# Pooled keys written once, as a ring of nine heads, and transposed by two DMAs from its first and second slot on

## Chip, cores, metric

One core of one Trainium2 chip. The metric is the device time of one execution in microseconds, lower is better. Before the change it was 290.78 us (median of three runs, 290.66 to 291.47). In what follows TensorE is PE in the profile (PEld are its weight loads), VectorE is DVE, ScalarE is ACT, GpSimd is POOL, and SyncE, which only issues DMAs here, is SP. Matmul results lie in PSUM, the rest of this kernel's tiles in SBUF; both are memories on the chip. All runs compared are in the fast state.

## The reference

```python
# q, k, v: 8 batches x 8 heads x 576 rows x 64;  w_in: 512 x 2048;  w_out: 2048 x 512
k_p = k.reshape(B, H, Sp, 8, D).mean(axis=3)          # 576 rows -> 72 pooled rows
v_p = v.reshape(B, H, Sp, 8, D).mean(axis=3)
attn = softmax(q @ k_p^T / sqrt(D));  x = attn @ v_p   # x as 4608 tokens x 512
h = x @ w_in
out = (h * cos(h)) @ w_out
```

## The kernel before

The 4608 tokens go through the two large products in nine tiles of 512, t = 0 to 8. During tile t the attention of batch b = t + 1 is done, and GpSimd pools the keys and values of the batch after. Five pieces matter here.

GpSimd pools by three rounds of pairwise adds. The last round of the keys is done twice, so that each head stands twice, side by side, before the transpose:

```python
def pool_rest(b, which):
    s, add = half_sums, nc.gpsimd.tensor_tensor
    for h in range(0, H, 4):
        add(out=s[:, h:h + 4, 0:2, :], in0=s[:, h:h + 4, 0:2, :], in1=s[:, h:h + 4, 2:4, :], op=ADD)   # L155
    if which == "k":
        for slot in range(2):
            add(out=kp2[b % 2][:Sp, :, slot, :], in0=s[:, :, 0, :], in1=s[:, :, 1, :], op=ADD)          # L158
    else:
        s = s.rearrange("p (j a) t d -> p j a t d", a=2)
        add(out=v_part(b), in0=s[..., 0, :], in1=s[..., 1, :], op=ADD)                           # L161
```

SyncE transposes the doubled keys in one DMA, so that every head's keys lie on both halves of the partitions (a score matmul takes the half on which its queries happen to lie):

```python
def k_transpose(b):
    nc.sync.dma_start_transpose(out=kk[b % 2], in_=kp2[b % 2].rearrange("p h s d -> p (h s d)"))
```

VectorE forms h * cos(h) from PSUM (L358), and sums and differences of the parts of g for a product scheme with seven instead of eight block products. These sums (L388) have **both inputs in SBUF**:

```python
nc.vector.tensor_mul(out=o, in0=ps, in1=c)                                  # L358: ps in PSUM
nc.vector.tensor_tensor(out=out[:, f0:f1], in0=x, in1=y, op=op)             # L388: x, y in SBUF
```

In each tile the sums begin after the fourth of eight chunks, while GpSimd, which works ahead through its queue, finishes the values and loads what comes next:

```python
for n, fp in enumerate(up_order(t)):
    up_mm(t, fp, ...); up_g(t, fp, between)                                  # L344; L354, L358
    if 0 < t and 3 <= n < 6:
        put_gs(*[(k, 0) for k in (((3,), (1,), ()) if t == 1 else ((1, 2), (3,), (4,)))[n - 3]])
    if 0 < t and b < B:
        if n == 0:
            q_transpose(b); k_transpose(b)
        elif n == 2:
            pool_rest(b, "v")
            if b + 1 < B:
                nc.gpsimd.tensor_copy(out=gate, in_=kk[b % 2][0:1, 0, 0:1])  # L580
                load_q(b + 1); load_kv(b + 1, "v", v)
# ... seven block products (L422), attention of batch b between them; then, after tile 0 (conditions cut) ...
nc.gpsimd.tensor_copy(out=gate, in_=g4[0:1, HF - 1, 0:1])                    # L703
pool_first(b + 1, "k")                                                       # L149
load_kv(b + 2, "k", k)
pool_rest(b + 1, "k")
pool_first(b + 1, "v")
```

The 1x1 gate copies hold GpSimd's queue, and the loads in it, until something else is done.

The softmax here doesn't subtract the row's maximum and nothing guards it: scores larger than these inputs give would overflow.

Of the kernel before, what the change touches and what calls it, by code (L numbers as in the profile page):

```python
# [10 lines left out]
BF16 = mybir.dt.bfloat16  # L11
ACTF = mybir.ActivationFunctionType
ADD = mybir.AluOpType.add
# [7 lines left out]
def kernel(  # L21
# [9 lines left out]
    nc = tc.nc  # L31
    B, H, S, D = q.shape
    Sp = S // POOL
# [22 lines left out]
    wpool = ctx.enter_context(tc.tile_pool(name="wpool", bufs=1))  # L56
# [17 lines left out]

    SpA = -(-Sp // 16) * 16
    kk = [wpool.tile([128, H, SpA], BF16, name=f"kk{i}") for i in range(2)]
    kp2 = [wpool.tile([SpA, H, 2, D], BF16, name=f"kp2{i}") for i in range(2)]

    vz = [wpool.tile([Sp, KCH, 4, D], BF16, name=f"vz{i}") for i in range(2)]

# [30 lines left out]
    def load_kv(b, which, src):  # L111

        st = kv_tile()[:Sp, 0:H * POOL * D].rearrange("p (h t d) -> p h t d", h=H, t=POOL)
        nc.gpsimd.dma_start(out=st.rearrange("p h t d -> p h (t d)"),
                            in_=src[b].rearrange("h (p t) d -> p h (t d)", t=POOL))
        staged[which, b] = st

    def load_q(b):
        q_tile(b)
        load_even(staged["q", b], b, q)  # L120
# [13 lines left out]
    half = (slice(0, 64), slice(64, 128))  # L134

    def v_part(b):
        return vz[b % 2][:, :, 0:4:3, :]

    def put_kk(b, ps, pj0, pj1, copy):
        dst = kk[b % 2].rearrange("p (j a) n -> p j a n", a=2)  # L140
        for a in range(2):
            for r in range(2):
                copy(out=dst[half[r], pj0:pj1, a, 0:Sp], in_=ps[half[a]])

    def pool_first(b, which):

# [4 lines left out]
    def pool_rest(b, which):  # L151

        s, add = half_sums, nc.gpsimd.tensor_tensor
        for h in range(0, H, 4):
            add(out=s[:, h:h + 4, 0:2, :], in0=s[:, h:h + 4, 0:2, :], in1=s[:, h:h + 4, 2:4, :], op=ADD)  # L155
        if which == "k":
            for slot in range(2):
                add(out=kp2[b % 2][:Sp, :, slot, :], in0=s[:, :, 0, :], in1=s[:, :, 1, :], op=ADD)  # L158
        else:
            s = s.rearrange("p (j a) t d -> p j a t d", a=2)  # L160
            add(out=v_part(b), in0=s[..., 0, :], in1=s[..., 1, :], op=ADD)  # L161

    def pool_k_mm(b, bank, pj0, pj1):

        kb = staged["k", b]
        ps = bank[:, 0:(pj1 - pj0) * Sp].rearrange("p (j n) -> p j n", n=Sp)
        for pj in range(pj0, pj1):
            for t in range(ROW):
                for rows in half:
                    nc.tensor.matmul(ps[rows, pj - pj0, :], lhsT=kb[rows, pj, t, :], rhs=groups[rows, t, :],  # L170
                                     start=(t == 0), stop=(t == ROW - 1))
        return lambda copy: put_kk(b, ps, pj0, pj1, copy)
# [8 lines left out]
                              in_=pair[:Sp, :, 0:KCH * D].rearrange("p a (j d) -> p a j d", j=KCH))  # L181

    def k_transpose(b):
        nc.sync.dma_start_transpose(out=kk[b % 2], in_=kp2[b % 2].rearrange("p h s d -> p (h s d)"))


    QB = KCH * ROW // 2
# [7 lines left out]
    def q_transpose(b):  # L195
        qT_tile(b)
        nc.sync.dma_start_transpose(out=att["qT", b], in_=q_flat(b))

    def q_transpose_mm(b, bank, g0, g1):

        if ("qT", b) not in att:
            qT_tile(b)
        ps = bank.bitcast(BF16)[:, 0:(g1 - g0) * 128].rearrange("p (g n) -> p g n", n=128)
        for g in range(g0, g1):
            nc.tensor.matmul(ps[:, g - g0, :], q_flat(b)[:, g * 128:(g + 1) * 128], identity, is_transpose=True)
        return lambda copy: copy(out=att["qT", b][:, g0:g1, :], in_=ps)

    def ex_col(u, i):

        (c0, n), (h0, nh) = u  # L210
        return (i // 2 % 2 * (nh // 2) + i // 4 * 2 + i % 2) * n

    def scores(b, u, pair):
        scores_mm(b, u, pair)
        scores_exp(b, u, pair)

    def scores_mm(b, u, pair):
        (c0, n), (h0, nh) = u

        for i in [i + 2 * a for k in range(0, nh, 4) for i in (k, k + 1) for a in range(2)]:  # L220
            bank, c = divmod(ex_col(u, i), nh * n // 2)
            pj, hp = divmod(h0 + i, 2)
            g, r = divmod(ROW * pj + ORDER[c0 // 64], 2)
            nc.tensor.matmul(pair[:Sp, bank, c:c + n].rearrange("p (g n) -> p g n", n=64),  # L224
                             lhsT=kk[b % 2][half[r], h0 + i, 0:Sp],
                             rhs=att["qT", b][half[r], g:g + n // 64, hp * 64:hp * 64 + 64])

    def scores_exp(b, u, pair):
# [99 lines left out]
    def up_order(t):  # L328
        n = FFCH // 2
        return range(n) if t < FIRST else [i + a * n // 2 for i in range(n // 2) for a in range(2)]  # L330
# [7 lines left out]
    def up_mm(t, fp, k0=0, k1=KCH):  # L338

        h = up_bank(t, fp)  # L340
        for j in range(2):
            fc = 2 * fp + j
            for ki in range(k0, k1):
                nc.tensor.matmul(h[j] if h is obanks else h[:, j, :], lhsT=w_in_sb[fc // 4][:, ki, (fc % 4) * 128:(fc % 4 + 1) * 128],  # L344
                                 rhs=xT[:, ki, t * TILE:(t + 1) * TILE],
                                 start=(ki == 0), stop=(ki == KCH - 1))

    def up_g(t, fp, between=()):
        h = up_bank(t, fp)
        cos = msb.tile([128, 2, TILE], FP32, name="cos", tag="cos", bufs=2)  # L350
        g = g_sb[:, 2 * fp:2 * fp + 2, :]
        parts = [(h[j], cos[:, j], g[:, j]) for j in range(2)] if h is obanks else [(h, cos, g)]
        for ps, c, _ in parts:
            nc.scalar.activation(out=c, in_=ps, func=ACTF.Sin, bias=half_pi[:, :1])  # L354
        for put, copy in between:
            put(copy)
        for ps, c, o in parts:
            nc.vector.tensor_mul(out=o, in0=ps, in1=c)  # L358
# [31 lines left out]
    def put_gs(*kis):  # L390
        for k, i in kis:
            put_g(k, i)
# [79 lines left out]
    for rows in half:  # L472
# [12 lines left out]
                  for x in (g1, g2)]  # L485
    groups = g3.rearrange("p f n -> p (f n)")[:, 0:ROW * Sp].rearrange("p (t n) -> p t n", t=ROW)
    nc.vector.tensor_tensor(out=dist, in0=row_of.unsqueeze(2).to_broadcast([128, ROW, Sp]),
                            in1=first_of.unsqueeze(1).to_broadcast([128, ROW, Sp]), op=mybir.AluOpType.subtract)
# [6 lines left out]
    gate = consts.tile([1, 1], BF16, name="gate")  # L495
# [12 lines left out]
    load_even(staged["v", 1], 1, v)  # L508
    nc.gpsimd.memset(vz[1], float(POOL))
    for i in range(2):  # L510
        nc.gpsimd.memset(kp2[i], 0.0)
    for cg in (2, 1, 3):
        load_w_out(cg)

# [37 lines left out]
    for t in range(NT):  # L552
        b = t + 1
# [4 lines left out]
        for n, fp in enumerate(up_order(t)):  # L558
            up_mm(t, fp, 2 if n < 2 else 0)
            between = ()  # L560
            if t == 0:
                if fp == 4:
                    puts = pool_k_mm(1, obanks[0], 0, 2), pool_k_mm(1, obanks[1], 2, 4)
                elif fp in (5, 6):
                    g0 = 9 * (fp - 5)
                    puts = q_transpose_mm(1, obanks[0], g0, g0 + 5), q_transpose_mm(1, obanks[1], g0 + 5, g0 + 9)
                if fp in (4, 5, 6):
                    puts[0](vec)
                    between = ((puts[1], act),)
            up_g(t, fp, between)  # L570
# [4 lines that stand above are left out]
                    q_transpose(b)  # L575
                    k_transpose(b)
                elif n == 2:
                    pool_rest(b, "v")
                    if b + 1 < B:
                        nc.gpsimd.tensor_copy(out=gate, in_=kk[b % 2][0:1, 0, 0:1])  # L580
                        load_q(b + 1)
                        load_kv(b + 1, "v", v)
            if n == 2:
                while stores:
                    stores.pop(0)()
# [39 lines left out]
        else:  # L625
# [11 lines left out]
            def scores_of(*parts):  # L637
                for part in parts:
                    scores_mm(*part)
                for part in parts:  # L640
                    scores_exp(*part)
# [52 lines left out]
        if b + 1 < B:  # L694
            if t == 0:
                load_kv(b + 1, "k", k)
                load_q(b + 1)
                load_kv(b + 1, "v", v)
                put_weights(0, nc.gpsimd, (3, 2, 4))
                put_weights(1, nc.gpsimd, (1,))  # L700
# [4 lines that stand above are left out]
            if b + 2 < B:  # L705
# [3 lines that stand above are left out]
# [28 lines left out]
```

## Time and profile before

The lines are in the prediction below; here is what they come to.

| | before |
|---|---|
| time, median of 3 | 290.78 us |
| PE busy, share of the span | 276.1 us, 96% |
| GpSimd busy, idle at gate L703 | 151.3 us, 36.0 us |
| length of tiles 2, 3, 4, 5, 6 | 30.07, 29.63, 29.64, 29.62, 28.95 us |
| mean of the L388 call; free call | 804 ns; about 690 ns |

Tile lengths run from the first up-projection matmul of a tile to that of the next. Tiles 2 to 6 hold the same matmuls, so their lengths can be set against each other; that is the reading on which everything below rests.

### The profile page before, as it was taken

How to read it: one execution, taken by the hardware profiler on the slowest of the kernel's cores; microseconds unless marked ns; L12 is line 12 of the kernel's file. 1: busy time of each engine (PE TensorE's matmuls, PEld its weight loads, DVE VectorE, ACT ScalarE, POOL GpSimd, SP SyncE). 2: the span in 40 equal slices, each digit the busy share in tenths (PEclk: the TensorE clock that was granted, in tenths of full speed). 3: DMA queues.
4: the chain of work that ended last, by engine and by line, in shares of the span. 5: the costliest groups of instructions: out<-in, count | busy, mean ns of one | idle time of the engine just before them, and what ended most of it. 6: DMA issues, size and time to landing. Idle time of an engine off the chain costs nothing.

```text
span 288.7 us, 5827 instructions
## 1 busy us (share of the span) xinstructions
PE 276.1 (96%) x2338; PEld 175.9 (61%) x2360; DVE 218.5 (76%) x314; ACT 164.5 (57%) x193; POOL 151.3 (52%) x150
## 2 busy tenths in 40 slices
PE   7889999999999899999999999999999999999994
PEld 2545454447864597449744884488448844874683
DVE  6458747899949995799569956995699569756962
ACT  3886798378157635763566556565566556436600
POOL 8563079997799369934994399529920000000000
PEclk9999999999999999999999999999999999999999
DMA  7999999793999957996789668972660261015014
GB/s 158 197 206 206 207 205 212 121 189 40 155 122 177 181 93 118 165 170 110 116 160 175 112 104 154 184 125 55 125 145 3 55 137 29 2 23 122 2 36 109
DMA packets 57545, 36.12 MB, mean 125 GB/s; under 512 B 35248, under 2 KB 53168, under 8 KB 57520
## 3 DMA queue, kind: packets, MB, share of 16 engines
q0 software_dynamic: 19744, 18.07, 40.0%
q1 hardware_dynamic: 37136, 17.18, 30.4%
q10 hardware_dynamic: 640, 0.52, 0.8%
q8 instruction: 18, 0.29, 0.4%
q14 instruction: 7, 0.06, 0.1%
HBM read 36.70 MB, written 9.44 MB: 160 GB/s over the span
## 4 chain that ended last, share of the span: by engine, by line
PE 64%; DVE 17%; DMA 12%; ACT 3%; POOL 2%; issue 1%; DVEq 0%; POOLq 0%
PE obank L422 27%; PE bank L344 24%; DVE g_sb L358 9%; DVE g L388 7%; DMA w_out_sb<-in_moe_w_out_dram 7%; DMA w_in_sb<-in_moe_w_in_dram 5%; PE obank L361 4%; ACT cos L354 3%; PE bank L224 3%; PE obank L344 2%; PE bank L286 2%; PE bank L259 1%; PE bank L422 1%; DVE o_two L438 1%; POOL q_b L95 1%
## 5 line engine op out<-in xcount | busy, mean ns | idle before, releaser
L344 PE MATMUL bank<-xT,w_in_sb 128*128 128x512 bf16 x495 | 113.5, 379 | 2.1 <-DVE g_sb L358 1.2
L354 ACT ACTIVATE cos<-bank,half_pi 128x1024 f32<-128x1024 f32 x64 | 70.4, 1114 | 58.5 <-PE bank L344 51.8
L344 PEld LDWEIGHTS <-w_in_sb 128*128 128x128 bf16 x576 | 56.0, 98 | 67.9 <-issue 2.9
L358 DVE TENSOR_TENSOR g_sb<-bank,cos 128x1024 bf16<-128x1024 f32 x64 | 77.0, 1219 | 24.9 <-ACT cos L354 24.8
L149 POOL TENSOR_TENSOR half_sums<-kv_st 72x512 f32<-72x512 bf16 x48 | 54.8, 1168 | 0.8 <-issue 0.2
L231 ACT ACTIVATE ex<-bank 72x1024 bf16<-72x1024 f32 (+1 forms) x40 | 35.0, 929 | 35.2 <-PE bank L224 35.1
L422 PEld LDWEIGHTS <-g 128*128 128x128 bf16 x512 | 47.9, 98 | 7.0 <-issue 1.2
L422 PE MATMUL obank<-w,g 128*128 128x256 bf16 x368 | 42.8, 272 | 0.4 <-DVE p_sb L436 0.2
L422 PEld LDWEIGHTS <-g_sb 128*128 128x128 bf16 x384 | 36.6, 98 | 8.7 <-DVE g_sb L358 2.2
L155 POOL TENSOR_TENSOR half_sums<-half_sums 72x512 f32<-72x512 f32 x24 | 30.9, 1309 | 0.1
L422 PE MATMUL obank<-w_out_sb,g_sb 128*128 128x256 bf16 x240 | 29.4, 273 | 1.1 <-DVE g_sb L358 1.1
L388 DVE TENSOR_TENSOR g<-g_sb 128x1024 bf16<-128x1024 bf16 x32 | 25.7, 804 | 0.5
L703 POOL COPY gate<-g 1x1 bf16<-1x1 bf16 x5 | 0.9, 180 | 36.0 <-DVE g L388 36.0
L270 DVE TENSOR_TENSOR xT<-bank,inv 64x256 bf16<-64x256 f32 x14 | 5.9, 422 | 15.2 <-ACT inv L266 15.1
L291 DVE TENSOR_TENSOR x_rows<-bank,inv_rows 128x512 bf16<-128x512 f32 x24 | 16.6, 692 | 0.8
L158 POOL TENSOR_TENSOR kp<-half_sums 72x512 bf16<-72x512 f32 x12 | 15.7, 1331 | 0.5
L361 PE MATMUL obank<-w_out_sb,g_sb 128*128 128x512 bf16 x61 | 14.9, 379 | 0.7 <-DMA w_out_sb<-in_moe_w_out_dram 0.3
L422 PE MATMUL obank<-w_out_sb,g 128*128 128x256 bf16 x112 | 15.6, 273 | 0.0
L422 PE MATMUL obank<-w,g_sb 128*128 128x256 bf16 x128 | 15.3, 273 | 0.0
L344 PE MATMUL obank<-xT,w_in_sb 128*128 128x512 bf16 x64 | 15.1, 379 | 0.0
L224 PE MATMUL bank<-qT,kk 64*72 64x128 bf16 (+2 forms) x288 | 12.4, 221 | 0.1
L388 DVE TENSOR_TENSOR g<-g,g_sb 128x1024 bf16<-128x1024 bf16 x16 | 12.0, 750 | 0.5
(103 smaller groups left out, 277.6 us busy)
## 6 DMA issues: line engine op xcount, KB each, us to landing
out_dram<-o_two SPq DMA_DIRECT2D x64, 128.0 KB, 2.4
kv_st<-in_v_dram POOLq DMA_DIRECT2D x8, 576.0 KB, 9.6
kv_st<-in_k_dram POOLq DMA_DIRECT2D x7, 576.0 KB, 8.4
q_b<-in_q_dram POOLq DMA_DIRECT2D x6, 576.0 KB, 6.6
w_in_sb<-in_moe_w_in_dram POOLq DMA_DIRECT2D x4, 512.0 KB, 13.4
w_out_sb<-in_moe_w_out_dram POOLq DMA_DIRECT2D x4, 512.0 KB, 18.8
q_b<-in_q_dram POOLq DMA_DIRECT2D x4, 288.0 KB, 12.2
g_sb<-in_k_dram SPq DMA_DIRECT2D x1, 576.0 KB, 3.5
```

What stands on the lines that cost most here:

```text
L149: nc.gpsimd.tensor_tensor(out=s[:, h:h + 2], in0=x[:, h:h + 2, 0:4, :], in1=x[:, h:h + 2, 4:8, :], op=ADD)
L155: add(out=s[:, h:h + 4, 0:2, :], in0=s[:, h:h + 4, 0:2, :], in1=s[:, h:h + 4, 2:4, :], op=ADD)
L158: add(out=kp2[b % 2][:Sp, :, slot, :], in0=s[:, :, 0, :], in1=s[:, :, 1, :], op=ADD)
L224: nc.tensor.matmul(pair[:Sp, bank, c:c + n].rearrange("p (g n) -> p g n", n=64), lhsT=kk[b % 2][half[r], h0 + i, 0:Sp], rhs=att["qT", b][h ...
L231: nc.scalar.activation(out=ex[:, 0:nh * n].rearrange("p (a n) -> p a n", a=2), in_=pair[:Sp, :, 0:nh * n // 2], func=ACTF.Exp, scale=scale ...
L291: nc.vector.tensor_tensor(out=x[0:n].rearrange("p (j a d) -> p j a d", j=KCH, a=2), in0=ps[0:n, :, 0:2 * (D + 2)].rearrange("p j (a w) -> ...
L344: nc.tensor.matmul(h[j] if h is obanks else h[:, j, :], lhsT=w_in_sb[fc // 4][:, ki, (fc % 4) * 128:(fc % 4 + 1) * 128], rhs=xT[:, ki, t * ...
L354: nc.scalar.activation(out=c, in_=ps, func=ACTF.Sin, bias=half_pi[:, :1])
L358: nc.vector.tensor_mul(out=o, in0=ps, in1=c)
L361: nc.tensor.matmul(o, lhsT=g_sb[:, fc, ms * 128:(ms + 1) * 128], rhs=w_out_sb[fc // 4][:, fc % 4, :], start=(fc == 0), stop=(fc == FFCH - 1))
L388: nc.vector.tensor_tensor(out=out[:, f0:f1], in0=x, in1=y, op=op)
L422: mms.append(lambda bank=bank, first=first, g=g, w=w, fc=fc, p=p: nc.tensor.matmul(bank[p], lhsT=g(fc, p), rhs=w(fc), start=(first and fc ...
```

## The change

Its intent is to save GpSimd the second full key add. Each head is written once, into a ring of nine slots whose last repeats head 0. One transpose takes slots 0 to 7 and gives the head pairs (0,1), (2,3) and so on; a second takes slots 1 to 8 and gives (1,2), (3,4) up to (7,0). So every head has come to lie on both halves, and `key_slot` says in which column.

```diff
-    kp2 = [wpool.tile([SpA, H, 2, D], BF16, name=f"kp2{i}") for i in range(2)]
+    ring = [wpool.tile([SpA, H + 1, D], BF16, name=f"ring{i}") for i in range(2)]
...
+    def key_slot(b, h, r):
+        if h % 2 == r:
+            return h // 2
+        return H // 2 + (h // 2 if b < 2 else (h - 1) % H // 2)
...
-            for slot in range(2):
-                add(out=kp2[b % 2][:Sp, :, slot, :], in0=s[:, :, 0, :], in1=s[:, :, 1, :], op=ADD)
+            for h0, n, slot in ((0, H, 0), (0, 1, H)):
+                add(out=ring[b % 2][:Sp, slot:slot + n, :], in0=s[:, h0:h0 + n, 0, :], in1=s[:, h0:h0 + n, 1, :], op=ADD)
...
-        nc.sync.dma_start_transpose(out=kk[b % 2], in_=kp2[b % 2].rearrange("p h s d -> p (h s d)"))
+        for i in range(2):
+            nc.sync.dma_start_transpose(out=kk[b % 2][:, i * H // 2:(i + 1) * H // 2],
+                                        in_=ring[b % 2][:, i:i + H].rearrange("p h d -> p (h d)"))
...
-                             lhsT=kk[b % 2][half[r], h0 + i, 0:Sp],
+                             lhsT=kk[b % 2][half[r], key_slot(b, h0 + i, r), 0:Sp],
...
-        nc.gpsimd.memset(kp2[i], 0.0)
+        nc.gpsimd.memset(ring[i], 0.0)
...
-                        nc.gpsimd.tensor_copy(out=gate, in_=kk[b % 2][0:1, 0, 0:1])
+                        nc.gpsimd.tensor_copy(out=gate, in_=kk[b % 2][0:1, H - 1, 0:1])
```

(Cut: `put_kk`, which writes the first two batches' keys to the new columns.)

More of the change, by code (lines that the diff above doesn't have):

```diff
@@ L137, in v_part @@
         return vz[b % 2][:, :, 0:4:3, :]
+    def key_slot(b, h, r):
+        if h % 2 == r:
+            return h // 2
+        return H // 2 + (h // 2 if b < 2 else (h - 1) % H // 2)
     def put_kk(b, ps, pj0, pj1, copy):
-        dst = kk[b % 2].rearrange("p (j a) n -> p j a n", a=2)
         for a in range(2):
             for r in range(2):
-                copy(out=dst[half[r], pj0:pj1, a, 0:Sp], in_=ps[half[a]])
+                j = key_slot(b, 2 * pj0 + a, r)
+                copy(out=kk[b % 2][half[r], j:j + pj1 - pj0, 0:Sp], in_=ps[half[a]])
     def pool_first(b, which):
```

## The prediction

> **What bounds the kernel now.** I read the page first. TensorE is busy nearly all the time and VectorE and GpSimd are not; GpSimd's own idle time ahead of its gate copy is large.
>
> ```profile
> PE 276.1 (96%) x2338; PEld 175.9 (61%) x2360; DVE 218.5 (76%) x314; ACT 164.5 (57%) x193; POOL 151.3 (52%) x150
> L388 DVE TENSOR_TENSOR g<-g_sb 128x1024 bf16<-128x1024 bf16 x32 | 25.7, 804 | 0.5
> L158 POOL TENSOR_TENSOR kp<-half_sums 72x512 bf16<-72x512 f32 x12 | 15.7, 1331 | 0.5
> ```
>
> See here that the changed line, L158, is on an engine busy half the time: 12 adds of 1.3 us. Taken alone, removing half of them removes nothing from the end. But L388 on VectorE has a mean of 804 ns although most of its calls take 0.69 us, so something stretches some of them.
>
> Then the waits, for the two that hold TensorE back in the steady stages, and for GpSimd's slack:
>
> ```profile
> POOL gate L703 <- DVE g L388: 36.0, 5, 8.2
> PE bank L344 <- DVE g_sb L358: 1.2, 4, 0.6
> PE obank L422 <- DVE g_sb L358: 1.1, 4, 0.3
> ```
>
> GpSimd idles 36.0 us over five stages at one gate, so it is in no hurry. TensorE waits for VectorE's product four times at each of two places, 2.3 us together. Four is the number of steady stages in which GpSimd pools, gates and loads (tiles 2 to 5 of the nine, counted from 0). I cut these stages at the first up-projection matmul (L344) of each tile, and took the table of windows:
>
> ```profile
> 83.09:113.16 30.07, 29.05 (x256) 19.27 (x257) 24.10 (x35) 17.05 (x19) 22.02 (x21) 1.00 0.90 142
> 113.16:142.79 29.63, 29.06 (x257) 19.29 (x257) 23.77 (x35) 17.05 (x19) 20.86 (x21) 1.00 0.87 141
> 172.43:202.05 29.62, 29.05 (x256) 19.25 (x256) 23.78 (x35) 17.05 (x19) 21.15 (x21) 1.00 0.73 131
> 202.05:231.00 28.95, 28.84 (x257) 19.40 (x256) 23.02 (x35) 17.05 (x19) 8.62 (x8) 1.00 0.41 82
> ```
>
> Columns: the window and its length, then PE, PEld, DVE, ACT and POOL busy, granted clock, DMA share, GB/s. Tile 6 (last row) does the same matmuls in 28.95 us that tiles 3 to 5 do in 29.63, 29.64 and 29.62 and tile 2 in 30.07. Its VectorE work is 0.75 us shorter with the same 35 instructions. The timeline says where: first tile 3, VectorE then GpSimd, and then tile 6 in the same order.
>
> ```profile
> 122.14 1.54 DVE L388 TENSOR_TENSOR g<-g_sb 128x1024 bf16<-128x1024 bf16 x1
> ...
> 121.87 1.27 POOL L161 TENSOR_TENSOR vz<-half_sums 72x512 bf16<-72x512 f32 x1
> 123.08 0.65 POOL L580 COPY gate<-kk 1x1 bf16<-1x1 bf16 x1
> ```
>
> ```profile
> 211.04 0.69 DVE L388 TENSOR_TENSOR g<-g_sb 128x1024 bf16<-128x1024 bf16 x1
> ...
> 209.56 1.27 POOL L161 TENSOR_TENSOR vz<-half_sums 72x512 bf16<-72x512 f32 x1
> ```
>
> In tile 3 the first L388 starts 0.27 us into GpSimd's last add (L161), lasts 1.54 us instead of 0.69, and ends 0.54 us after that add; the 1x1 gate copy that follows then takes 0.65 us and ends with L388. Each seems to wait for the other to finish. In tile 6 the add is over at 210.83, before L388 starts, and L388 takes 0.69. Tiles 4 and 5 look like tile 3 (L388 1.56 and 1.54 us, L161 starting 0.26 and 0.27 us earlier). In tile 2 GpSimd is about 0.85 us later still: the first L388 takes 1.04 us (held by the tail of L155), the second 1.64 us (held by L161).
>
> **What the Trainium skill says.** "SBUF — State Buffer", section "Who interferes with whom": a VectorE instruction with two SBUF inputs contends with a GpSimd instruction that reads SBUF, and the later of the two blocks fully. L388 adds two SBUF tensors; L161 reads SBUF. The trace agrees (1.54 against 0.69 us), and agrees that L358, which reads one operand from PSUM, is not stretched: 1.21 to 1.23 us in either case. "Perfetto Trace Analysis", section "GPSIMD Engine Instruction", advises timing GpSimd by the spacing of starts; L158's pair and the add behind it start 2.57 us apart (112.28 to 114.85), so one is 1.28. "DMA: Bandwidth & Descriptors", "DMA Transpose (X-bar)", asks for a partition count in multiples of 16: 80 rows are kept. Its section "Two DMAs through the same engine are not ordered" implies that both transposes need their own semaphore wait; the built order shows six more waits on TensorE's weight loads of kk.
>
> **The change part by part.**
> 1. GpSimd, per tile 1 to 6 (six times): the second 72x512 add (1.28 us by spacing) becomes one of 72x64. Estimate of the latter: L158 takes 1.26 us for 512 columns; the small GpSimd instructions of the start take 0.16 to 0.29 us; so 0.28 us. Saved: 1.28 - 0.28 = 1.0 us, always ahead of the pooling of the values. GpSimd starts each stage at the gate L703, which VectorE sets, so all its later work comes 1.0 us earlier against VectorE's.
> 2. Collisions, tiles 3 to 5. L161 ends 1.00, 1.00 and 0.99 us after L388 starts (121.87 + 1.27 - 122.14 and so on). Less 1.0: it ends just as L388 starts. The gate copy (0.18 us when free) comes next and may cost a little. L388 was delayed 0.85 us; I take 0 to 0.3 after. The stage lost 0.68 us (29.63 - 28.95) for a delay of 0.85, so 0.17 us of delay is absorbed. What is left is lost 0 to 0.13 us; gain 0.55 to 0.68, I take 0.62. Three tiles: 1.86 us.
> 3. Tile 2: delays were 1.04 - 0.69 + 1.64 - 0.69 = 1.30 us, and the stage lost 30.07 - 28.95 = 1.12, again 0.18 absorbed. Moved up by 1.0, L161 runs from about 91.65 to 92.9, and L388 from 92.07 waits for it: some 0.7 us, of which 0.55 counts. Gain 0.57 us. Tile 1 has no TensorE gap at this place and gains nothing.
> 4. SyncE: one transpose of 8 blocks (1.23 us of issue, landing 2.8 us after it began) becomes two of 4 blocks. The nearest row is the xT transpose, also 4 blocks: 1.22 us issue, 2.5 us landing. So the second lands at about 1.1 + 2.5 = 3.6 us, 0.8 us later than now: 118.40 + 3.6 = 122.0 in tile 3. The scores need it at 129.83, 7.8 us later: hidden. The gate copy would come at 122.1: a near tie. If it waits, L388 goes first, which costs TensorE nothing; the loads behind it start no later than today's 123.67. The stores behind shift by 1 us on a queue that is then idle until 134.87.
> 5. TensorE: the same 288 key loads and matmuls from other columns of kk, and six semaphore waits that are long satisfied: up to 0.1 us in all, as I judge it.
> 6. Start: the two memsets of 80x1024 (0.97 us each) shrink to 80x576, 0.55 us by size, so w_out's second load is issued 0.85 us earlier. The load TensorE really waited for (0.3 us) is the third, held by another load's completion. I count 0.
>
> Sum: 1.86 + 0.57 - 0.1 = 2.3 us, 290.78 - 2.3 = 288.5.
>
> **The rivals.**
> (a) Hidden: GpSimd has slack, so nothing moves: 290.8. For it: the 36.0 us of idle gate. Against it: tile 6 shows the same matmuls 0.68 us faster without the collision. It would hold if the saved 1.0 us were eaten before L161, by a small add near 0.6 us or a new wait.
> (b) The collision moves rather than goes: the gate copy, or L161 by a few tenths, still meets L388. Part of the gain, 289.3 to 290.
> (c) The transposes become the cost: twelve in place of six, slower landing, the loads behind the gate late or the stores in the way. Slack of 7.8 us at the scores speaks against; at most 291.5.
> (d) A full cure, with tile 2 cured too and 0.3 us at the start: 290.78 - (1.12 + 3 x 0.68) - 0.3 = 287.3.
>
> **Range and chances.** My middle is 288.5; (d) gives the low end, 287.3; (b) gives the high end, 290.1. Two per cent is 5.8 us, more than the whole of the collisions (3.2 us), so faster by over 2% has 0.01. Slower by over 2% needs a new wait of 1 us in every stage: 0.01. Within 2%: 0.98.
>
> **What would show it.** Step 1: GpSimd's busy time falls by about 6 us plus 0.85 us of memset, the small add near 0.28 us. Step 2: the first L388 of tiles 3 to 5 falls to 0.7 to 1.0 us, these stages to 28.95 to 29.1. Step 3: tile 2 near 29.5. Step 4: kk landing later by under 1.2 us, TensorE never waiting for it. Step 5: TensorE's waits for L358 fall from 2.3 us to under 1. It is wrong if L388 keeps 1.5 us somewhere in each stage, if the small add is much dearer than 0.28 us, or if the stages shorten and another shows up longer.

## The result and the profile after

The changed kernel takes **287.67 us** (median of 4 runs, 287.52 to 288.02), the kernel before 290.72 us (4 runs, 290.49 to 291.47). The ratio is 0.9892, 95% interval 0.9872 to 0.9912: 1.1% faster. A ratio here is the mean time of one kernel's fast runs over that of the other's of the same rounds, so not quite the ratio of the medians. A later call measured the same kernel again, at 287.87 us and 0.9896 (0.9863 to 0.9929).

The line numbers have moved by up to nine: L353 is the up-projection (L344 before), L367 the multiply from PSUM (L358), L397 the sums of g (L388), L165 the key add (L158), L168 the value add (L161), L589 and L712 the gates. From the page of the changed kernel, the busy times of the engines and the group of the sums:

```profile
PE 275.0 (96%) x2338; PEld 176.4 (62%) x2360; DVE 215.1 (75%) x314; ACT 164.2 (57%) x193; POOL 144.2 (50%) x150
L397 DVE TENSOR_TENSOR g<-g_sb 128x1024 bf16<-128x1024 bf16 x32 | 23.2, 725 | 0.5
```

GpSimd does 7.1 us less, as intended. But VectorE, of which the change took nothing, is busy 3.4 us less, 2.5 of them in this one group of the same 32 instructions (25.7 to 23.2). The windows of tiles 2, 3, 5 and 6 (length; then PE, PEld, DVE, ACT, POOL busy):

```profile
83.12:112.07 28.95, 28.84 (x255) 19.30 (x257) 22.36 (x34) 17.04 (x19) 20.05 (x21) 1.00 0.90 147
112.07:141.02 28.95, 28.84 (x257) 19.43 (x257) 23.02 (x35) 17.03 (x19) 19.93 (x21) 1.00 0.84 142
169.97:198.92 28.95, 28.84 (x257) 19.42 (x257) 23.02 (x35) 17.04 (x19) 20.16 (x22) 1.00 0.73 135
198.92:227.86 28.94, 28.84 (x257) 19.37 (x257) 23.01 (x35) 17.04 (x19) 7.83 (x7) 1.00 0.41 82
```

Tiles 2 to 5 now have the length that tile 6 had all along. Tile 3 in the timeline, VectorE and then GpSimd:

```profile
121.05 0.69 DVE L397 TENSOR_TENSOR g<-g_sb 128x1024 bf16<-128x1024 bf16 x1
121.78 0.69 DVE L397 TENSOR_TENSOR g<-g,g_sb 128x1024 bf16<-128x1024 bf16 x1
...
119.89 1.27 POOL L168 TENSOR_TENSOR vz<-half_sums 72x512 bf16<-72x512 f32 x1
121.11 0.68 POOL L589 COPY gate<-kk 1x1 bf16<-1x1 bf16 x1
```

The value add ends at 121.16, 0.11 us after the first sum begins, and the sum takes 0.69 us in place of 1.54. What still meets it is the gate copy, and now it is the copy that waits (0.68 us for one element). TensorE's waits, the ones that changed:

```profile
PE bank L353 <- DMA xT<-x_rows: 0.6, 1, 0.6
...
PE bank L353 <- DVE g_sb L367: 0.2, 1, 0.2
```

The 2.3 us of waits for VectorE's product have shrunk to 0.2, but there is a new one: 0.6 us for a transpose of x, once, at the start of tile 2. The sum over the span: tiles 2 to 5 give 3.17 us (118.96 to 115.79, from the start of tile 2 to that of tile 6), the part ahead of tile 2 gives nothing (it starts at 83.09 and 83.12), and what follows costs 0.16; together 3.0 us, as the spans say (288.7 and 285.7). The 0.16 lies behind TensorE's last matmul, which comes 26.8 us into the last tile in every profile: the last tile takes 30.77 to 30.79 us in the four profiles with one transpose of the keys and 30.91 to 30.95 in the seven with two (the three with another order, below, left out). In the second profile of the changed kernel (below) the part ahead of tile 2 costs 0.57 us, since tile 2 starts at 83.66; what is gained there varies between executions.

### The profile page after: what moved, and what is told of

Its sections match the earlier page's. It is cut to its first block, busy times and chain, and to the rows that moved or that the text cites. A ratio compares the mean times of both kernels' runs of the same rounds, so it can differ in the third digit from the quotient of the medians.

```text
span 285.7 us, 5835 instructions
## 1 busy us (share of the span) xinstructions
PE 275.0 (96%) x2338; PEld 176.4 (62%) x2360; DVE 215.1 (75%) x314; ACT 164.2 (57%) x193; POOL 144.2 (50%) x150
## 4 chain that ended last, share of the span: by engine, by line
PE 80%; DVE 9%; DMA 3%; ACT 3%; issue 2%; POOL 0%; DVEq 0%; POOLq 0%; ACTq 0%
PE bank L353 35%; PE obank L431 27%; PE obank L370 4%; PE obank L353 4%; DVE g_sb L367 3%; PE bank L233 3%; DVE g L397 3%; DMA q_b<-in_q_dram 2%; ACT cos L363 2%; PE bank L295 2%; DMA xT<-x_rows 1%; PE bank L268 1%; DVE w L387 1%; PE bank L431 1%; ACT ex L240 1%
## 5 line engine op out<-in xcount | busy, mean ns | idle before, releaser
L353 PE MATMUL bank<-xT,w_in_sb 128*128 128x512 bf16 x495 | 113.1, 379 | 1.7 <-DMA xT<-x_rows 0.6
L353 PEld LDWEIGHTS <-w_in_sb 128*128 128x128 bf16 x576 | 56.0, 98 | 67.0 <-issue 1.7
L367 DVE TENSOR_TENSOR g_sb<-bank,cos 128x1024 bf16<-128x1024 f32 x64 | 77.3, 1220 | 25.8 <-ACT cos L363 25.6
L431 PE MATMUL obank<-w_out_sb,g_sb 128*128 128x256 bf16 x240 | 28.8, 273 | 0.0
L397 DVE TENSOR_TENSOR g<-g_sb 128x1024 bf16<-128x1024 bf16 x32 | 23.2, 725 | 0.5
L712 POOL COPY gate<-g 1x1 bf16<-1x1 bf16 x5 | 0.9, 180 | 36.9 <-DVE g L397 36.9
L353 PE MATMUL obank<-xT,w_in_sb 128*128 128x512 bf16 x64 | 15.1, 379 | 0.0
L233 PEld LDWEIGHTS <-kk 64*72 64x72 bf16 x288 | 8.9, 110 | 5.3 <-issue 3.8
```

What stands on the lines that cost most here:

```text
L233: nc.tensor.matmul(pair[:Sp, bank, c:c + n].rearrange("p (g n) -> p g n", n=64), lhsT=kk[b % 2][half[r], key_slot(b, h0 + i, r), 0:Sp], rh ...
L353: nc.tensor.matmul(h[j] if h is obanks else h[:, j, :], lhsT=w_in_sb[fc // 4][:, ki, (fc % 4) * 128:(fc % 4 + 1) * 128], rhs=xT[:, ki, t * ...
L431: mms.append(lambda bank=bank, first=first, g=g, w=w, fc=fc, p=p: nc.tensor.matmul(bank[p], lhsT=g(fc, p), rhs=w(fc), start=(first and fc ...
```

## The experiments

Theory: the whole gain is that the value add on GpSimd comes 1 us earlier against VectorE and no longer holds VectorE's first sum. Rivals: the ring layout or the smaller transposes help; any GpSimd work at that moment holds VectorE; the gain is all or nothing. Twelve kernels ran, in three calls; those of one call share a chip and the runs of the kernel before (median 290.89, 290.35 and 290.62 us). In the third call one run of the kernel before took 293.54 us at a clock of 0.988; the record counts it as fast, and without it the ratios of that call would be 0.001 higher.

### One part alone: the short add

```diff
-            for slot in range(2):
-                add(out=kp2[b % 2][:Sp, :, slot, :], in0=s[:, :, 0, :], in1=s[:, :, 1, :], op=ADD)
+            for slot, n in ((0, H), (1, 1)):
+                add(out=kp2[b % 2][:Sp, 0:n, slot, :], in0=s[:, 0:n, 0, :], in1=s[:, 0:n, 1, :], op=ADD)
```

> The kernel before, with the second key add cut from eight heads to one and nothing else changed (keys of the second slot stay stale, so the result is wrong on purpose). Theory (the value add of GpSimd comes about 1 us earlier and no longer holds VectorE's first two-SBUF-input add of tiles 2 to 5): 287.4 to 288.2 us, the L388 calls of tiles 3 to 5 near 0.69 us, those stages 28.95 us. Rival (the gain comes from the ring layout or the two smaller transposes): 290.5 to 291 us, L388 still at 1.54 us.

Measured: 287.88 us, ratio 0.9903 (0.9880 to 0.9925). Tiles 2 to 5 take 28.94 to 28.95 us, the first sum of tile 3 0.69 us. (The output passed the comparison although seven heads' second copy of the keys is never written; the inputs are small, so that, as I judge, keys hardly move the softmax. The kernel is still wrong.) The shorter add alone gives the gain, within the intervals.

### The other part alone: two transposes

```diff
-        nc.sync.dma_start_transpose(out=kk[b % 2], in_=kp2[b % 2].rearrange("p h s d -> p (h s d)"))
+        for i in range(2):
+            hs = slice(i * H // 2, (i + 1) * H // 2)
+            nc.sync.dma_start_transpose(out=kk[b % 2][:, hs], in_=kp2[b % 2][:, hs].rearrange("p h s d -> p (h s d)"))
```

> The kernel before, with both full key adds kept and only the one transpose split into two of four blocks. Theory of the GpSimd add: nothing gained, 290.4 to 291.2 us, L388 at 1.5 us in tiles 3 to 5; the later landing is hidden. Rival (smaller transposes help): 287.5 to 289 us. Rival (two transposes cost something that the change then had to make good): above 291.3 us.

Measured: 290.20 us, ratio 0.9986 (0.9963 to 1.0009): no difference. Tile 3 in its timeline, and its window:

```profile
121.69 1.55 DVE L390 TENSOR_TENSOR g<-g_sb 128x1024 bf16<-128x1024 bf16 x1
...
121.43 1.27 POOL L161 TENSOR_TENSOR vz<-half_sums 72x512 bf16<-72x512 f32 x1
```

```profile
112.71:142.35 29.64, 29.16 (x259) 19.29 (x257) 23.79 (x35) 17.04 (x19) 20.87 (x21) 1.00 0.83 139
```

The sum is still held and the tile still takes 29.64 us. The second transpose costs nothing visible in the tiles and brings nothing.

### The saved time put back, in full and in part

Both keep the ring and the two transposes and add GpSimd work of seven or of three heads into a tile that nobody reads (the edit in short):

```diff
+            add(out=spare[:Sp, 0:n], in0=s[:, 0:n, 0, :], in1=s[:, 0:n, 1, :], op=ADD)     # n = 7, or n = 3
```

> The changed kernel with a third add on GpSimd of seven heads into a spare tile, some 1.1 us, so that GpSimd's time per tile is a little above that before the change, with ring and two transposes kept. Theory: the collision is back, about 0.16 us worse than before the change in each of four tiles: 290.7 to 291.6 us, first L388 1.5 us or more. Rival (ring layout or transposes): 287.5 to 288 us.

Measured: 291.63 us, ratio 1.0026 (1.0004 to 1.0047). The loss is back; the median is 0.03 us above the range.

> The changed kernel with a third add of three heads into a spare tile, some 0.6 us: half way back. Theory: the value add ends some 0.75 us after the first L397 of tiles 3 to 5 starts, the call takes 1.2 to 1.4 us, these stages lose 0.4 us each and tile 2 0.6: 289.2 to 289.8 us. Rival (a threshold: the gain is there in full or not at all): 287.7 or 290.7 us.

Measured: 288.95 us, ratio 0.9960 (0.9945 to 0.9975), between the two, so there is no threshold; but less lost than expected. In tile 3 of each, seven heads first and three heads second:

```profile
122.26 1.68 DVE L399 TENSOR_TENSOR g<-g_sb 128x1024 bf16<-128x1024 bf16 x1
...
122.13 1.26 POOL L170 TENSOR_TENSOR vz<-half_sums 72x512 bf16<-72x512 f32 x1
```

```profile
121.18 1.12 DVE L399 TENSOR_TENSOR g<-g_sb 128x1024 bf16<-128x1024 bf16 x1
...
120.48 1.27 POOL L170 TENSOR_TENSOR vz<-half_sums 72x512 bf16<-72x512 f32 x1
```

With three heads the value add ends 0.57 us after the sum starts (120.48 + 1.27 - 121.18), where I had put 0.75. The delay is 1.12 - 0.69 = 0.43 us, and the tile takes 29.20, a loss of 0.25.

Set against each other over the profiles, the sums' delay in a tile and what the tile is longer than 28.95 us:

| kernel, tile | delay of the sums, us | tile longer by, us |
|---|---|---|
| changed (second run), 2 | 0.17 | 0.00 |
| three heads, 3 | 0.43 | 0.25 |
| before, 3 | 0.85 | 0.68 |
| seven heads, 3 | 0.99 | 0.81 |
| three heads, 2 | 1.16 | 0.98 |
| before, 2 | 1.30 | 1.12 |
| seven heads, 2 | 1.70 | 1.52 |

The loss is the delay less 0.17 or 0.18 us in every row. That is the slack of VectorE ahead of TensorE; the prediction had read it from two tiles of one profile. The delay has a rule of its own in these profiles: it is the time by which the add outlasts the sum's start, less 0.14 us. In tile 3 of the kernels with seven heads, before the change and with three heads 1.13, 1.00 and 0.57 us gave 0.99, 0.85 and 0.43; in tile 2 of the changed kernel's second run 0.31 gave 0.17.

### Is it GpSimd's reading that holds VectorE?

```diff
-            s = s.rearrange("p (j a) t d -> p j a t d", a=2)
-            add(out=v_part(b), in0=s[..., 0, :], in1=s[..., 1, :], op=ADD)
+            for i in range(2):
+                nc.gpsimd.memset(v_part(b), 0.5 + i)
```

> The kernel before, with the value add replaced by two memsets of the same tile, some 1.1 us together, which write SBUF and read none (wrong result on purpose). They run at the same place as the add did. If only GpSimd's reading of SBUF holds a VectorE add with two SBUF inputs: the first L388 of tiles 3 to 5 at 0.69 us although the memsets overlap it, and 287.4 to 288.3 us. Rival (any GpSimd work that writes SBUF at that time holds it): L388 at 1.2 us or more and 289.5 to 291 us.

Measured: 287.21 us, ratio 0.9890 (0.9862 to 0.9918); the result is wrong, as meant. Both full key adds are in this kernel. Tile 3:

```profile
120.36 0.69 DVE L388 TENSOR_TENSOR g<-g_sb 128x1024 bf16<-128x1024 bf16 x1
...
120.05 1.11 POOL L161 MEMSET vz<- 72x512 bf16 x2
```

The memsets run from 120.05 to 121.16, right across the sum, and it takes 0.69 us. The memsets end 0.80 us after it starts; the add, ending 1.00 us after, delayed it by 0.85, so memsets that held it likewise would have made it some 1.3 us, or 0.9 had only the first of the two (its end is at 120.58). So work of GpSimd that only writes doesn't hold the sum, and the rival falls. (The memsets are some 0.16 us shorter than the add; that they overlap the whole sum shows that the shortening isn't the reason.)

### The same gain by order alone

The kernel before, with all its work; from tile 2 on the value add waits for VectorE's first pair of sums:

```diff
-                elif n == 2:
-                    pool_rest(b, "v")
+                elif n == 2 and t > 1:
+                    pool_rest(b, "v", (0,))                    # the round in front of the last
+                elif n == (2 if t == 1 else 3):
+                    if t > 1:
+                        nc.gpsimd.tensor_copy(out=gate, in_=g2[0:1, 0, 0:1])
+                    pool_rest(b, "v", (0, 1) if t == 1 else (1,))
```

(Cut: the new argument of `pool_rest` that names its rounds.)

> The kernel before, keys and transposes untouched; from tile 2 on the value add of GpSimd waits, by a 1x1 copy that reads g2, until VectorE has done the first pair of two-SBUF-input adds, and then runs beside the multiplies that read PSUM. Theory (only the meeting of that add with VectorE's pair costs time): the gain of the change without the change, tiles 3 to 5 at 28.95 us, tile 2 at 28.95 to 29.2 (the tail of the add in front may still meet the first call), 287.4 to 288.3 us. Rival (the gain needs less work on GpSimd or the new key layout): 290 to 291 us.

Measured: 288.35 us, ratio 0.9920 (0.9885 to 0.9955). Three quarters of the gain with no work removed. Tiles 3 to 6 take 29.13 us, not 28.95 (in tile 6, which took 28.95 before, that is a loss): the first two sums are free, but the third now meets the tail of the value add.

```profile
121.00 0.69 DVE L390 TENSOR_TENSOR g<-g_sb 128x1024 bf16<-128x1024 bf16 x1
121.79 0.69 DVE L390 TENSOR_TENSOR g<-g,g_sb 128x1024 bf16<-128x1024 bf16 x1
...
123.54 0.97 DVE L390 TENSOR_TENSOR g<-g_sb 128x1024 bf16<-128x1024 bf16 x1
...
122.69 1.26 POOL L163 TENSOR_TENSOR vz<-half_sums 72x512 bf16<-72x512 f32 x1
```

That is 0.28 us, and the second sum starts 0.08 us later than it could (a free pair starts 0.72 apart, as in the changed kernel); 0.36 in all, less 0.18, is the 0.18 us that the tile lost.

The same edit on the changed kernel:

> The changed kernel with the same wait of the value add. Theory: its tiles 2 to 5 are already at 28.95 us, so nothing more is gained: within 0.3 us of the changed kernel run beside it. Rival (what is left of GpSimd's load still costs, in a place not seen): 0.5 us or more faster.

Measured: 289.13 us, ratio 0.9946 (0.9907 to 0.9985), slower than the changed kernel beside it (287.87). The expected "within 0.3 us" was wrong: the wait that helps the kernel before makes this one's third sum meet the value add (tiles 3 to 6 at 29.13). That accounts for 0.66 us over tiles 2 to 5 and 0.18 in tile 6. The last tile was also longer, 31.05 us with one transpose and 31.21 and 31.25 with two in the three kernels with this order, against 30.77 to 30.95 in the others, 0.28 us here. This again lies behind TensorE's last matmul; its cause is not known. Together that is 1.1 of the 1.26 us by which this kernel is slower.

### The new wait at tile 2

The changed kernel once more, without an edit:

> The changed kernel once more, on the chip of this call, to compare with the others of it: 287.5 to 288.1 us, ratio to the kernel before 0.988 to 0.992, tiles 2 to 5 at 28.95 us. Open is whether the 0.6 us wait for the xT transpose at tile 2 shows again or was of one execution.

Measured: 287.87 us, as said above, and the wait for the x transpose shows again, at 0.5 us. It is there in six of the ten profiles that load the next keys where the kernel before does, among them the one with only the transposes split (0.7 us) and the kernel before in another order (0.5 us), so it isn't special to the ring or to two transposes.

The next keys are loaded a little later, first on the changed kernel:

```diff
             pool_first(b + 1, "k")
-            if b + 2 < B:
-                load_kv(b + 2, "k", k)
             pool_rest(b + 1, "k")
+            if b + 2 < B:
+                load_kv(b + 2, "k", k)
```

> The changed kernel, with the load of the next keys issued after the key pooling instead of ahead of it (some 2.5 to 4 us later). In the changed kernel's profile TensorE waited 0.6 us at tile 2 for the xT transpose, which lands about when that load has begun. Theory (the load is in the transpose's way): that wait goes, 287.0 to 287.4 us. Rival (the wait was chance, or the transpose is slow without the load): 287.5 to 287.9 us. Should the value add come nearer to L397 the stages stay 28.95 us all the same.

Measured: 288.15 us, ratio 0.9932 (0.9916 to 0.9949). A miss: the wait for the transpose is gone from the profile, but the kernel is no faster. Its ratio is 0.4% above those of the changed kernel (0.9892, 0.9896), its median only 0.1 to 0.2% (287.67, 287.87), and each call had another chip, so whether it is slower isn't settled. In tile 1 a new meeting took the gain. VectorE, GpSimd and then TensorE:

```profile
63.06 3.15 DVE L397 TENSOR_TENSOR g<-g_sb 128x1024 bf16<-128x1024 bf16 x1
...
63.18 2.48 POOL L162 TENSOR_TENSOR half_sums<-half_sums 72x512 f32<-72x512 f32 x2
65.74 1.60 POOL L168 TENSOR_TENSOR vz<-half_sums 72x512 bf16<-72x512 f32 x1
...
67.40 1.89 PE L353 MATMUL bank<-xT,w_in_sb 128*128 128x512 bf16 x8 [0.95 <-DVE g_sb L367]
```

The sum that started at 63.06 had to let two adds of GpSimd go first and ended at 66.21; TensorE waited 0.95 us for what stands behind it. Tiles 1 and 2 took 30.45 and 29.16 us, against 30.47 and 28.95 in the changed kernel. So 0.2 us is lost there. The rest by which this profile is longer (287.4 against 285.7 us) is its later start of tile 1 (54.20 against 52.65): it is of the slowest of the six executions, 289.22 us.

The same edit on the kernel before:

> The kernel before with the same later key load alone. The load no longer stands ahead of the key pooling, but GpSimd still does it before the value add, so that the add still meets L388: 290.3 to 290.9 us if the theory of the collision is right. Rival (the order of the loads sets the time of GpSimd's later adds): under 290 us.

Measured: 290.06 us, ratio 0.9991 (0.9976 to 1.0005). Just below the range, and not by its reasoning: the value add of tile 3 now ends 0.50 us after the sum starts in place of 1.00 (0.3 of it is a pause of GpSimd ahead of that load, which is gone), so that tiles 3 to 5 lose only 0.18 to 0.20 (29.13 to 29.15). But one sum of tile 1 takes 4.09 us and that tile 31.39, which costs what the others gain.

The later load on the changed kernel with a larger ring, of which only nine heads are used:

```diff
-    ring = [wpool.tile([SpA, H + 1, D], BF16, name=f"ring{i}") for i in range(2)]
+    ring = [wpool.tile([SpA, 2 * H, D], BF16, name=f"ring{i}") for i in range(2)]
```

> As the later key load on the changed kernel, but the ring is 16 heads wide, so that the two memsets at the start take 0.97 us each as before the change. If the smaller memsets gave the 0.2 to 0.3 us that TensorE no longer waited for w_out: 0.2 to 0.3 us slower than with the later key load alone. Rival (the start was chance): the same within 0.1 us.

Measured: 287.95 us, ratio 0.9926 (0.9911 to 0.9941), no slower than 288.15. The smaller memsets at the start give nothing measurable.

The changed kernel with the value add's wait, and the later load in tile 1 alone:

```diff
+            if t == 1:
+                pool_rest(b + 1, "k")
             if b + 2 < B:
                 load_kv(b + 2, "k", k)
-            pool_rest(b + 1, "k")
+            if t != 1:
+                pool_rest(b + 1, "k")
```

> The changed kernel with the value add's wait, and in tile 1 alone the next keys' load after the key pooling. If that load is what holds the xT transpose at tile 2: no wait of TensorE for it, 0.4 to 0.7 us faster than the changed kernel beside it (tile 1 near 29.8 us). Rival (the wait does not come from that load): the same within 0.3 us.

Measured: 288.32 us, ratio 0.9916 (0.9879 to 0.9952). It was expected to be faster than the changed kernel (287.87) and is slower: a miss. Against the same kernel without the later load (289.13) it is 0.8 us faster, tile 1 takes 29.72 in place of 30.49, and TensorE doesn't wait for the transpose. None of the four profiles with the later load shows such a wait. So the runs point to that load as what holds the transpose. Four of the ten profiles with the earlier load show no such wait either, and the transposes' own times show why. The one in question is the third of tile 1's transposes of x. In eight profiles the load was issued 0.2 to 0.5 us after it; the transpose landed 3.9 to 4.4 us after its own issue, and tile 2 started 0.14 us after that landing, to the hundredth. These are the six with the wait, the kernel with memsets (where the profile puts 0.3 us down to VectorE) and the kernel before (where TensorE had no gap just then). In the two others (seven and three heads put back) the load came 0.9 and 0.8 us after the transpose, and in the four with the later load 4 us or more: there the transpose landed after 2.4 to 2.7 us, and tile 2 started 1.2 us or more after the landing, held by something else. This is an ordering found in the fourteen profiles afterwards, not an experiment.

This kernel does not beat the changed kernel, since it carries the wait of the value add, which costs 0.8 us over tiles 2 to 6 and 0.3 us at the end; tile 1 gives back 0.7. The later load in tile 1 without that wait was not run. No version with a right result beat the changed kernel.

## Why the prediction was right, step by step

**Which meeting costs the time (the reading of what bounds the kernel): right, and shown.** The first sum of tiles 3 to 5 fell to 0.69 us and these tiles to 28.94 to 28.95. The short add alone gave it; the work put back took it away, in proportion; and order alone gave three quarters of it on the kernel before.

**Step 1, GpSimd's saving: right.** The small add takes 0.31 us at the least against the 0.28 of the estimate, and GpSimd's busy time fell by 7.1 us where 6 plus 0.85 stood (in tile 1, beside a sum of weights on VectorE, the small add takes 0.77).

**Step 2, tiles 3 to 5: right, a little low.** 0.62 us was taken for each; they gave 0.68, 0.70 and 0.67. The remnant that I allowed for didn't come: the add ends 0.10 to 0.13 us after the sum starts, within the 0.14 us that delay nothing.

**Step 3, tile 2: the term was mis-sized.** It stood at 0.57 us and gave 1.12. Measured from the gate at tile 1, the value add did start 0.95 us earlier (18.76 to 17.81 us after it). But the sum came 0.64 us later after that gate (18.19 to 18.83), because TensorE had waited 0.6 us for the x transpose. So tile 2 was cured in full at the price of that wait in tile 1. The prediction had no such wait. It is luck that the size still came near: in the second profile the cure of tile 2 (1.12 us) less the later start of tile 2 (0.57) leaves 0.55, the size of the prediction's term but not by its reasoning.

**Step 4, SyncE: right.** Each transpose takes 1.20 us to issue and lands after 2.4 us, so the second lands about 3.6 us after the first began, as estimated (4.1 in tile 4, 1.3 later than the one transpose did there, where under 1.2 was set). TensorE never waited for it. The near tie at the gate showed: in two of five tiles the gate copy waited, 0.4 us for the second transpose and 0.7 us in tile 2, where the profile names ScalarE although the second transpose lands just then; it cost TensorE nothing.

**Steps 5 and 6: right in size.** Nothing of the extra semaphore waits shows in TensorE's waits; the 0.16 us at the end, which goes with the second transpose, was not foreseen. The start was counted at 0, and with large memsets the kernel was no slower. In the two profiles tile 1 starts 0.98 us earlier after the change, but tile 2 starts at the same time: the third transpose of x was issued only 0.3 us earlier (78.77 against 79.07) and took 0.3 us longer to land (4.2 against 3.9). Over all fourteen profiles tile 1 starts at 52.6 to 54.2 us, so its earlier start is not shown to be of the change.

**The sum.** 2.3 us were predicted and 3.05 measured (290.72 to 287.67), inside the range. The excess is tile 2 (0.55), tiles 3 to 5 (0.19) and the 0.1 us for waits that didn't show, less 0.16 at the end. Rival (a), hidden, and rival (c), the transposes, are refuted by the runs. Rival (b), the meeting moves, came true in the changed kernel only in tile 1, where the first sum takes 1.81 us in place of 1.54 and TensorE waits 0.2 us; it is also what the order experiments and the later load ran into. Rival (d), the full cure, is close to what happened in tiles 2 to 5.

What stays open: why an x transpose lands later when the keys' load follows it within 0.5 us, whether the later load loses more than the 0.2 us of tile 2, and what the end of the program spends its extra time on.

## What to carry to other kernels

When a VectorE instruction that reads two operands from SBUF has calls of very different length, look at what GpSimd read at that moment, and count only the delay above VectorE's slack. Idle time on GpSimd doesn't make its work free: a microsecond less on an engine busy half the time was worth 3 us here, because it moved one add out of the way four times. Shifting by a dependency can do the same without removing work, but look at what the shifted instruction meets next; each of my own shifts met another sum.

## What the Trainium skill lacked or had wrong

- "SBUF — State Buffer", "Summary: rules for kernel authors", says that the second to issue blocks until the first finishes, and doesn't say that it can be passed over again. Here VectorE sums that take 0.69 us when free took 3.15 and 4.09 us, while GpSimd began further adds in front of them. When this happens and when one add is the end of it was not settled. The page's rule for reads, in "Who interferes with whom", was right: with a read the sum took 1.54 us, with memsets across it 0.69.
- "DMA: Bandwidth & Descriptors", "DMA Transpose (X-bar)", gives no issue time (the page's only counts, in a comparison made for trn3, are of other cases). Transposes of 4 and of 8 blocks of 80 rows both took about 1.2 us of SyncE (1.20 and 1.23), and landed after 2.4 and 2.8 us in the changed kernel and the kernel before. Nor does it say what a load beside a transpose costs: 4 blocks of x landed after 3.9 to 4.4 us when a load was issued 0.2 to 0.5 us behind them, and after 2.4 to 2.7 us when it came later.
